# A gated attention and convolution layer on one core: four output tiles summed in one bank, wider evictions, longer parameter rows, and a new written order

## The chip, the core and the metric

The kernel runs on one core of a Trainium2 chip. The core has a matrix engine (TensorE, "PE" in the profile, its weight loads "PEld"), a vector engine (VectorE, "DVE"), a scalar engine (ScalarE, "ACT"), GpSimd ("POOL"), SyncE ("SP", which here only issues transfers) and 16 DMA engines. Matmuls write PSUM, a small memory of 8 banks; VectorE or ScalarE must copy each result out of it (an *eviction*) before the bank can be used again. The metric is the device time of one execution in microseconds; lower is better.

## The reference, cut to what matters

```python
x = A_x                                            # (1, 2048, 512), bf16
g = sigmoid((x * gate_w).sum(-1, keepdims=True))
a = A(x)                                           # attention, 32 heads of 16, four segments of 512 tokens
b = B(x)                                           # long convolution, one filter of 2048 taps per channel
return g * a + (1 - g) * b

# A, segment s:  p = softmax(causal(q k^T / 4));  a_dot = p v
#   num, den = phi(q) M, phi(q) z                  # memory of the earlier segments
#   o = sigmoid(beta) * num / (den + 1e-6) + (1 - sigmoid(beta)) * a_dot
#   M, z += phi(k)^T v, sum phi(k);   A = concat(o) @ wo
# B:  dt = exp(log_dt);  K[d, l] = Re sum_n C B dt exp(dt * (A_re + i A_im) * l)
#   y = irfft(rfft(x, 4096) * rfft(K, 4096))[:2048] + x * Dskip
```

## The kernel before

The convolution is a two-level Fourier transform written as matmuls. `x_level1` (L867) loads x in four parts of 512 KB, one for each group of four residues b of the token number modulo 16, multiplies each of the 16 blocks by a constant matrix in two halves, each half in a PSUM bank of its own, copies each half out (32 evictions of 512 columns), and stores the result to a scratch tensor in DRAM, `scr_Z`. `tail` runs twice, once for each half of the channels ("a", "b"), and for 16 frequency groups t it loads constants and the scratch, does the second level (X), multiplies it by the transform of the filter (K, then Y on VectorE), and transforms back (V). After the 16 groups, `fir` (eight pairs of residues) does the last level and the Dskip term by matmul, and evicts 512 columns a pair into a buffer `cv`. `final` (L1358) makes one output tile per residue b (128 tokens b, b+16, ...): four matmuls of the attention result with wo, then one VectorE instruction that adds `cv` times (1 - g), then the store.

The filter comes from `ssm_prep` (six parameter loads, transposed on the PE and evicted as `prm`, L766; exp, sine and cosine), `ssm_powers` (ten squarings, L816 to L826), and `tables(c)` for four channel groups: products of powers on VectorE (`cmul`, three VectorE instructions a call, L1188, L1191, L1195) and short matmuls ("lag"). The attention goes by segment s and head group hg: `project` (pk, pq), `seg_tokens` (values; L941 sets a column of ones), `seg_state` (the memory), `scores` (five groups of scores a head group; each fills four PSUM banks, and one ScalarE exp of 2048 columns at L1091 reads them), `pv`, and `ophase` (memory read, transposition "oT"). The gate g is folded into the scale of each token's attention result, through `oms` and `einvT`.

Every piece of work is an `op` with an engine; plain copies ("ANY") may go to ScalarE (L226) or VectorE (L227). Almost all matmuls show as L695, and all plain transfers as L222. Nothing is scheduled on the chip: `ORDER` is a string written out by hand or by a planner, and `replay` turns it into one instruction list for each engine:

```python
for w in ORDER.split():
    w = w.split("/")
    order.append((int(w[0].rstrip("av")), "ACT" if w[0][-1] == "a" else "DVE", [int(v) for v in w[1:]]))
```

The number is the op in the order in which `build_graph` makes it, the suffix is the engine of an "ANY" op (a ScalarE, v VectorE), and the numbers after the slashes are the buffer slots or banks that it takes. Each engine works through its list in order; `emit` adds a wait for every operand and for the earlier users of a slot. The transfers of one engine are issued in its order too, so a transfer that waits holds up those behind it. SBUF areas are shared over time: a pool of a later phase waits for the pools that lay there before.

## Time and profile before

| | us |
|---|---|
| three runs: median (lowest to highest) | 313.13 (312.26 to 315.39) |
| the profiled execution | 316.78 |
| its span, first to last instruction | 315.0 |
| PE busy / DVE busy / ACT busy | 275.4 / 268.7 / 260.2 |
| POOL busy | 8.3 |

The rows of a profile are read like this. A group row has the source line, the engine, the operation, output and input, the shape, the count, the busy time, the mean length of one, and the idle time of the engine just before with what ended it. The chain of waits starts at the last instruction and goes back, at each step, to what released it. A window row has, for a stretch of the span, each engine's busy time, the granted clock of the PE, the DMA engines' share and their rate. Lengths are of one instruction from start to end; two that follow each other on ScalarE overlap a little, so the distance from start to start is shorter.

### The profile page before, as it was taken

Reading aid. Unit: us, or ns where it says so; the run is one execution under the profiler, and the core shown is the slowest. Engines: PE = TensorE matmul, PEld = TensorE weight load, DVE = VectorE, ACT = ScalarE, POOL = GpSimd, SP = SyncE. Lnnn points to the kernel's source line nnn. Section 1 sums busy time; section 2 is a strip of 40 time slices with the busy share of each in tenths; the row PEclk is TensorE's granted clock in tenths of the full one; section 3 lists DMA queues with packets and bytes.
Section 4 is the critical chain, followed back from the end, with each engine's and each line's share of the span. In section 5 each row is a group of like instructions: output and inputs, shape, how many; then the busy total and the mean of one; then the engine's idle time right before and its main releaser. Section 6 shows DMA issues by size and latency. Waiting matters only on the chain.

```text
span 315.0 us, 10488 instructions
## 1 busy us (share of the span) xinstructions
PE 275.4 (87%) x4459; PEld 193.6 (61%) x4459; DVE 268.7 (85%) x650; ACT 260.2 (83%) x307; POOL 8.3 (3%) x18
## 2 busy tenths in 40 slices
...
GB/s 182 244 157 88 147 155 207 103 33 35 121 85 191 89 83 103 156 172 91 204 173 193 138 165 198 184 162 214 174 279 191 226 251 218 101 21 2 3 175 93
DMA packets 52289, 45.70 MB, mean 145 GB/s; under 512 B 22337, under 2 KB 47570, under 8 KB 52242
## 3 DMA queue, kind: packets, MB, share of 16 engines
...
q10 hardware_dynamic: 674, 0.16, 0.2%
...
HBM read 26.79 MB, written 6.29 MB: 105 GB/s over the span
## 4 chain that ended last, share of the span: by engine, by line
PE 40%; ACT 28%; DVE 14%; DMA 7%; issue 7%; SPq 3%; ACTq 0%; DVEq 0%
PE psum L695 39%; ACT sb L1091 15%; ACT sb L226 8%; DVE sb L1373 3%; DMA sb<-sb 3%; SPq L222 3%; ACT sb L816 2%; DMA sb<-scr_Z 2%; DMA sb<-in_B_A_im_dram 2%; DVE sb L227 2%; DVE sb L1195 1%; DVE sb L1191 1%; DVE sb L1320 1%; ACT sb L969 1%; DVE sb L1228 1%
## 5 line engine op out<-in xcount | busy, mean ns | idle before, releaser
L695 PE MATMUL psum<-sb 128*128 128x17 bf16 (+15 forms) x4341 | 266.9, 226 | 26.5 <-ACT sb L1091 12.9
L695 PEld LDWEIGHTS psum<-sb 128*128 128x128 bf16 (+5 forms) x4341 | 184.4, 100 | 104.6 <-ACT sb L1091 23.9
L1091 ACT ACTIVATE sb<-psum 128x2048 bf16<-128x2048 f32 x80 | 152.5, 1906 | 9.6 <-PE psum L695 8.7
L226 ACT ACTIVATE sb<-psum 128x512 bf16<-128x512 f32 (+3 forms) x157 | 91.7, 645 | 18.4 <-PE psum L695 17.9
L227 DVE CAST sb<-psum 128x512 bf16<-128x512 f32 (+1 forms) x64 | 43.4, 689 | 14.0 <-PE psum L695 13.7
L1320 DVE TENSOR_TENSOR sb<-sb 128x1024 bf16<-128x1024 bf16 x32 | 21.7, 683 | 5.4 <-ACT sb L226 2.8
L1188 DVE TENSOR_TENSOR sb<-sb 128x512 bf16<-128x512 bf16 (+4 forms) x44 | 24.7, 564 | 0.2
L1191 DVE TENSOR_TENSOR sb<-sb 128x512 bf16<-128x512 bf16 (+4 forms) x44 | 24.6, 562 | 0.2
L1103 DVE TENSOR_TENSOR sb<-sb 128x1024 bf16<-128x1024 bf16 (+1 forms) x40 | 22.5, 577 | 2.4 <-ACT sb L1091 2.4
L1195 DVE TENSOR_TENSOR sb<-sb 128x512 bf16<-128x512 bf16 (+4 forms) x44 | 23.8, 548 | 0.5
L1066 DVE TENSOR_TENSOR sb<-psum,sb 128x256 bf16<-128x256 f32 x32 | 13.3, 419 | 0.5
L1373 DVE SCALAR_TENSOR_TENSOR sb<-sb,psum 128x512 bf16<-128x512 bf16 x16 | 10.6, 740 | 2.3 <-PE psum L695 2.3
L816 ACT ACTIVATE sb<-sb 128x512 f32<-128x512 f32 x18 | 12.4, 686 | 0.0
L1228 DVE TENSOR_TENSOR sb<-sb 128x2048 bf16<-128x2048 bf16 x8 | 9.5, 1221 | 0.1
L227 DVE COPY sb<-psum 128x1024 bf16<-128x1024 bf16 x4 | 2.7, 680 | 7.5 <-PE psum L761 7.5
L1223 DVE TENSOR_TENSOR sb<-sb 128x4096 bf16<-128x4096 bf16 x4 | 9.1, 2282 | 0.0
L969 ACT ACTIVATE sb<-psum 128x512 bf16<-128x512 bf16 x12 | 7.6, 632 | 1.7 <-PE psum L966 1.7
L1063 DVE RECIPROCAL sb<-psum 128x16 f32<-128x16 f32 x32 | 8.0, 251 | 0.9 <-PE psum L695 0.9
L1143 DVE TENSOR_TENSOR sb<-psum,sb 128x512 bf16<-128x512 f32 x12 | 8.3, 688 | 0.3
L1020 ACT ACTIVATE sb<-sb 128x512 bf16<-128x512 bf16 x12 | 7.6, 636 | 0.0
L818 DVE SCALAR_TENSOR_TENSOR sb<-sb 128x256 f32<-128x256 f32 x18 | 7.4, 413 | 0.1
L817 DVE TENSOR_TENSOR sb<-sb 128x256 f32<-128x256 f32 x18 | 7.4, 412 | 0.1
...
## 6 DMA issues: line engine op xcount, KB each, us to landing
...
sb<-scr_Z SPq DMA_DIRECT2D x32, 128.0 KB, 3.1
sb<-sb SPq DMA_DIRECT2D x32, 128.0 KB
...
out_dram<-sb SPq DMA_DIRECT2D x16, 128.0 KB, 1.7
```

The source lines that it names most:

```text
L226: fa = lambda e: e.activation(dst(), src(), ACT.Copy)
L227: fd = lambda e: e.tensor_copy(dst(), src())
L695: mm = lambda e, o_, l, r_, st, sp, **kw: e.matmul(o_, lhsT=l, rhs=r_, start=st, stop=sp, skip_group_check=True, **kw)
L816: op("ACT", ("As", 512), lambda e, sq=sq, Z=Z: e.activation(ap(sq, n=512), ap(Z, n=512), ACT.Square), r=[Z], w=[sq], key=PW[h] + PWS * k)
L1066: op("DVE", ("V1", 256), lambda e: e.tensor_tensor(ap(o1, gi * 16, [[128, 4], [32, 4], [1, 16]]), ap(T, dims=[[68, 4], [17, 4], [1, 16]]), ...
L1091: o = op("ACT", ("Ax", 2048), lambda e, P=P, pT=pT: e.activation(ap(pT, n=2048), ap(P, n=2048), ACT.Exp, scale=0.25), r=[P], w=[pT])
L1103: op("DVE", ("V2", 128 * nb), lambda e, pT=pT, dims=dims: e.tensor_tensor(ap(pT, dims=dims + [[1, 128]]), ap(pT, dims=dims + [[1, 128]]), ...
L1188: op("DVE", ("V2" if n > 1 else "V1", 256 * n), lambda e: e.tensor_tensor(run(tile, ne, dst, 1), run(tile, ne, src, sstep), zz(cl * 512), ...
L1191: op("DVE", ("V2" if n > 1 else "V1", 256 * n), lambda e: e.tensor_tensor(run(t2, n, 0, 1), run(tile, ne, src, sstep), zz(cl * 512 + 256), ...
L1195: op("DVE", ("V2" if n > 1 else "V1", 256 * n), lambda e: e.tensor_tensor(D_(), D_(), ap(t2, n * 128, [[-n * 128, 2], [2 * n, 64], [1, 2 * ...
L1320: op("DVE", ("V2", 1024), lambda e, Y=Y, XAB=XAB, K3=K3: e.tensor_tensor(ap(Y, dims=[[512, 2], [1, 512]]), ap(XAB, dims=[[512, 2], [1, 512 ...
L1373: op("DVE", ("V1", 512), lambda e: e.scalar_tensor_tensor(ap(ou, n=512), ap(cv, (b % 2) * 512, n=512), ap(omgT, b, n=1), ap(P, n=512), ALU ...
```

## The change

1. **Four output tiles in one bank.** For b = 12 to 15 (`DIRECT`) `fir` is left out; `final` first runs the convolution matmuls of both halves into the tile's bank, then the four attention matmuls on top, and one plain copy with the scale (1 - g) writes the tile. It may run on ScalarE or VectorE. So that the scale is right, the gate of these tokens becomes g / (1 - g): `einvT` adds a column of `mkT` (0 for these tokens, 1 for the others) in place of 1.0. `cv` has six slots in place of eight; `ou` has 9 in place of 21, since it no longer reaches into the area of V2a.
2. **Two-bank evictions.** Both halves of a first-level block go to one tile of two neighbouring banks, and one copy of 1024 columns takes them out: 16 evictions in place of 32.
3. **Parameters in 1 KB rows.** Partition p takes the four channels 4p to 4p+3 in one row of 1 KB, where it took four rows of 256 B; the eviction of the transposed parameters puts the channels in order, by reading PSUM with a step.
4. **First x in parts.** The first of the four loads of x becomes four of 128 KB, two from SP and two from ACT.
5. **Smaller edits.** Each `pv` waits for its own part of the values and the ones, not for all four parts. For s = 0 the transposition "oT" writes bf16 to PSUM. `F_EXP` is reordered, so that the filter tables have two products of two in place of one of one and one of three.
6. **New order.** `ORDER` is replaced as a whole (1810 ops where there were 1843); of the copies, 146 go to ScalarE (167 before) and 103 to VectorE (98 before).

```diff
+DIRECT = (12, 13, 14, 15)
...
-8/0 10/4 18/0 12/0 11/4 0/0 13/1 1247/0 6/0 34/4 35/0 28/0/0 29v 37/0 38/1 44/2 9/1 26/0 36/3 45/4 60/1 1265/0/0
+13/0 8/0 10/4 12/1 9/4 213/0 0/0 1250/0 28/4/0 18/0 6/0 1248 29v 1249 34/5 35/0 36/0 37/1 1254/0/0 1255a 44/2 39/3
...
-F_EXP = [1, 2, 3, 4, 5, 6, 7, 8, 258, 260, 262, 264, 516, 520, 772, 776, 1032, 1288, 1544, 1800]
+F_EXP = [1, 5, 7, 3, 6, 4, 8, 2, 262, 260, 264, 258, 516, 520, 772, 776, 1032, 1288, 1544, 1800]
...
-    mkT = cload((pidx // 16) % 2 == 1, "mk", F32, 4, q="POOL")
+    mkT = cload(np.stack([(pidx // 16) % 2 == 1, np.isin(pidx % 16, DIRECT, invert=True)], 1), "mk", F32, 4, q="POOL")
...
-    cvP = mkpool("cv", 2048, 8, 3)
+    cvP = mkpool("cv", 2048, 8 - len(DIRECT) // 2, 3)
...
-    ouP = mkpool("ou", 1024, (T0 - a) // 1024, 3)
-    assert a <= T0, a - T0
+    ouP = mkpool("ou", 1024, (H2 - a) // 1024, 3)
+    assert a <= H2, a - H2
...
-        S.dma(lambda T=T: ap(T, dims=[[128, 4], [1, 128]]), lambda wi=wi: prm[wi].rearrange("(k p) n -> p k n", p=128),
+        S.dma(lambda T=T: ap(T, n=512), lambda wi=wi: prm[wi].rearrange("(p k) n -> p (k n)", k=4),
...
-            S.evac(lambda T=T: ap(T, n=1024), lambda P=P: ap(P, n=1024), 1024, r=[P], w=[T], psum16=True)
+            S.evac(lambda T=T: ap(T, dims=[[512, 2], [4, 128], [1, 4]]), lambda P=P: ap(P, dims=[[512, 2], [1, 128], [128, 4]]), 1024, r=[P], w=[T])
...
-            S.dma(lambda xj=xj: ap(xj, n=2048), lambda qd=qd: bass.AP(x.tensor, x.offset + qd * 2048, [[8192, 128], [1, 2048]]),
-                  524288, w=[xj], key=S.key + qd * XLS - 6)
+            xq = [xj]
+            if qd == 0:
+                xq = [xj.part() for _ in range(4)]
+                for bl in range(4):
+                    S.tag = "xl1l%d.%d" % (qd, bl)
+                    S.dma(lambda xj=xj, bl=bl: ap(xj, bl * 512, n=512), lambda bl=bl: bass.AP(x.tensor, x.offset + bl * 512, [[8192, 128], [1, 512]]),
+                          131072, w=[xq[bl]], key=S.key - 6, q="ACT" if bl > 1 else "SP")
+            else:
+                S.dma(lambda xj=xj: ap(xj, n=2048), lambda qd=qd: bass.AP(x.tensor, x.offset + qd * 2048, [[8192, 128], [1, 2048]]),
+                      524288, w=[xj], key=S.key + qd * XLS - 6)
...
-                for hf in range(2):
-                    P = S.ps()
-                    op("PE", c_pe("F", 512), lambda e, P=P, xj=xj, bl=bl, hf=hf: mm(e, ap(P, n=512), ap(W1T, hf * 128, n=128), ap(xj, bl * 512, n=512), True, True),
-                       r=[xj, W1T], w=[P], acq=[zs], key=S.key + (b4 / 4) * XLS)
-                    S.evac(lambda zs=zs, hf=hf: ap(zs, hf * 256, [[512, 2], [1, 256]]), lambda P=P: ap(P, dims=[[256, 2], [1, 256]]), 512, r=[P], pw=[zs], key=S.key + (b4 / 4) * XLS)
+                P = S.ps(2)
+
+                def f1(e, P=P, xj=xj, bl=bl):
+                    for hf in range(2):
+                        i = mm(e, ap(P, hf * 512, n=512), ap(W1T, hf * 128, n=128), ap(xj, bl * 512, n=512), True, True)
+                    return i
+                op("PE", c_pe("F", 512, 512), f1, r=[xq[bl % len(xq)], W1T], w=[P], acq=[zs], key=S.key + (b4 / 4) * XLS)
+                S.evac(lambda zs=zs: ap(zs, dims=[[256, 2], [512, 2], [1, 256]]), lambda P=P: ap(P, dims=[[512, 2], [256, 2], [1, 256]]), 1024,
+                       r=[P], w=[zs], key=S.key + (b4 / 4) * XLS)
...
-        op("DVE", ("V1", 4), lambda e: e.tensor_scalar_add(g(einvT), g(expT), 1.0), r=[expP[s]], w=[einvP[s]])
+        op("DVE", ("V1", 4), lambda e: e.tensor_scalar(g(einvT), g(expT), ap(mkT, 1, n=1), None, ALU.add), r=[expP[s], mkT], w=[einvP[s]])
...
+        vone = vp.part()
...
-        op("POOL", ("G", 128), lambda e: e.memset(ap(vp, 16, [[17, 128], [1, 1]]), 1.0), pw=[vp])
+        op("POOL", ("G", 128), lambda e: e.memset(ap(vp, 16, [[17, 128], [1, 1]]), 1.0), w=[vone])
...
-            S.evac(lambda tb=tb: ap(vp, tb * 544, [[17, 32], [1, 16]]), lambda P=P: ap(P, dims=[[16, 32], [1, 16]]), 512, r=[P], pw=[pt, vp])
+            S.evac(lambda tb=tb: ap(vp, tb * 544, [[17, 32], [1, 16]]), lambda P=P: ap(P, dims=[[16, 32], [1, 16]]), 512, r=[P], w=[pt])
...
-        vpad[s] = (vp, vparts)
+        vpad[s] = (vp, vparts + [vone])
...
-        op("PE", c_pe("F", *[136] * 8), f, r=[vp, ek, rk], pw=[PS], acq=[Mx[s + 1]])
+        op("PE", c_pe("F", *[136] * 8), f, r=vpad[s][1] + [ek, rk], pw=[PS], acq=[Mx[s + 1]])
...
-            op("PE", c_pe("F", *[17] * (4 * (4 - J))), f, r=[pT, vparts[J], vp], pw=[T])
+            op("PE", c_pe("F", *[17] * (4 * (4 - J))), f, r=[pT, vparts[J], vparts[4]], pw=[T])
...
-        P3 = S.ps()
+        P3 = S.ps(dt=F32 if s else BF16)
...
+                    if s == 0:
+                        i = e.transpose(ap(P3, tb * 128, n=128), ap(T, tb * 128, n=128), ap(ident, n=128))
+                        continue
...
-        S.evac(lambda: ap(oTT[0], hg * 2048 + 512 * s, n=512), lambda: ap(P3, n=512), 512, r=[P3], pw=[pt])
+        S.evac(lambda: ap(oTT[0], hg * 2048 + 512 * s, n=512), lambda: ap(P3, n=512), 512, r=[P3], pw=[pt], psum16=s == 0)
...
-        for e_, k_ in ((0, 0), (1, 1), (3, 2), (7, 3)):
+        for e_, k_ in ((0, 0), (7, 1), (5, 2), (6, 3)):
...
-        fm(2, 0, 1, 1, 1)
+        fm(3, 0, 5, 2, 1)
...
-        fm(4, 0, 1, 3, 2)
+        fm(1, 0, 3, 2, 2)
...
-        fm(8, 1, 2, 4, 8)
-        fm(12, 3, 4, 2, 9)
-        fm(14, 9, 2, 2, 9)
+        fm(8, 4, 1, 4, 8)
+        fm(12, 5, 1, 2, 9)
+        fm(14, 9, 1, 2, 9)
...
+    convs = []
...
+        def conv(e, P, c0, b, st, sp):
+            for kt in range(2):
+                i = mm(e, ap(P, c0, n=256), ap(G2T, kt * 128, n=128), ap(V2, (b * 2 + kt) * 256, n=256), st and kt == 0, False)
+            for kk in range(2):
+                k = 2 * half + kk
+                i = mm(e, ap(P, c0 + kk * 128, n=128), ap(xTT[0], k * 2048 + b, [[16, 128]]), ap(diagT, k * 128, n=128), False, sp and kk == 1)
+            return i
+        convs.append((conv, V2))
...
+            bs = [b for b in (2 * g2, 2 * g2 + 1) if b not in DIRECT]
+            if not bs:
+                continue
...
+            nb = len(bs)
...
-            def f2(e, P=P, b0=2 * g2):
-                for j in range(2):
-                    for kt in range(2):
-                        i = mm(e, ap(P, j * 256, n=256), ap(G2T, kt * 128, n=128), ap(V2, ((b0 + j) * 2 + kt) * 256, n=256),
-                               j == 0 and kt == 0, False)
-                for j in range(2):
-                    for kk in range(2):
-                        k = 2 * half + kk
-                        i = mm(e, ap(P, j * 256 + kk * 128, n=128), ap(xTT[0], k * 2048 + b0 + j, [[16, 128]]), ap(diagT, k * 128, n=128),
-                               False, j == 1 and kk == 1)
+            def f2(e, P=P, bs=bs):
+                for j, b in enumerate(bs):
+                    i = conv(e, P, j * 256, b, j == 0, b == bs[-1])
...
-            op("PE", c_pe("F", *[256] * 4 + [128] * 4), f2, r=[G2T, V2, diagT] + xTT, w=[P], acq=[cv])
-            S.evac(lambda cv=cv: ap(cv, half * 256, [[512, 2], [1, 256]]), lambda P=P: ap(P, dims=[[256, 2], [1, 256]]), 512, r=[P], pw=[cv])
+            op("PE", c_pe("F", *[256, 256, 128, 128] * nb), f2, r=[G2T, V2, diagT] + xTT, w=[P], acq=[cv])
+            S.evac(lambda cv=cv, nb=nb: ap(cv, half * 256, [[512, nb], [1, 256]]), lambda P=P, nb=nb: ap(P, dims=[[256, nb], [1, 256]]), 256 * nb, r=[P], pw=[cv])
...
-        cv = cvs[b // 2]
+        direct = b in DIRECT
+        k = b // 2
...
-            return mm(e, ap(P, n=512), ap(oTT[0], hg * 2048 + b, [[16, 128]]), ap(woT, hg * 512, n=512), hg == 0, hg == 3)
+            return mm(e, ap(P, n=512), ap(oTT[0], hg * 2048 + b, [[16, 128]]), ap(woT, hg * 512, n=512), hg == 0 and not direct, hg == 3)
...
-        op("PE", c_pe("F", *[512] * 3), f, r=[woT] + [oTp[(s, hg)] for s in range(4) for hg in range(3)], w=[P], acq=[ou])
+
+        def fc(e):
+            for half in range(2):
+                i = convs[half][0](e, P, half * 256, b, half == 0, False)
+            return i
+        if direct:
+            op("PE", c_pe("F", *[256, 256, 128, 128] * 2), fc, r=[G2T, convs[0][1], convs[1][1], diagT] + xTT, w=[P], acq=[ou])
+        o = op("PE", c_pe("F", *[512] * 3), f, r=[woT] + [oTp[(s, hg)] for s in range(4) for hg in range(3)], **({"pw": [P]} if direct else {"w": [P], "acq": [ou]}))
...
-        op("DVE", ("V1", 512), lambda e: e.scalar_tensor_tensor(ap(ou, n=512), ap(cv, (b % 2) * 512, n=512), ap(omgT, b, n=1),
-                                                                ap(P, n=512), ALU.mult, ALU.add), r=[P, omgT, cv], w=[ou])
+        if direct:
+            S.evac(lambda: ap(ou, n=512), lambda: ap(P, n=512), 512, r=[P, omgT], w=[ou], scale=lambda: ap(omgT, b, n=1))
+        else:
+            cv = cvs[k]
+            j = [b_ for b_ in (2 * k, 2 * k + 1) if b_ not in DIRECT].index(b)
+            op("DVE", ("V1", 512), lambda e: e.scalar_tensor_tensor(ap(ou, n=512), ap(cv, j * 512, n=512), ap(omgT, b, n=1),
+                                                                    ap(P, n=512), ALU.mult, ALU.add), r=[P, omgT, cv], w=[ou])
...
```

179 lines of the change are left out of this document (89 added, 90 removed).

## The prediction

> **What bounds the kernel now.** I read the stages first: one row for each stretch, with busy time of PE, PEld, DVE, ACT and POOL.
>
> ```profile
> 0.00:24.00 24.00, 17.21 (x131) 10.63 (x131) 15.59 (x47) 16.08 (x30) 6.98 (x16) 1.00 0.79 193
> 24.00:100.00 76.00, 63.11 (x1304) 39.84 (x1304) 75.31 (x199) 75.82 (x93) 0.66 (x1) 0.98 0.46 111
> 100.00:226.00 126.00, 115.33 (x1946) 83.59 (x1946) 105.21 (x251) 106.23 (x127) 0.65 (x1) 0.97 0.56 159
> 226.00:282.50 56.50, 55.59 (x796) 42.50 (x796) 50.08 (x110) 51.62 (x53) 0.00 (x0) 1.00 0.63 185
> 282.50:292.00 9.50, 8.29 (x165) 6.42 (x164) 8.74 (x23) 8.00 (x5) 0.00 (x0) 1.00 0.01 2
> 292.00:309.40 17.40, 15.84 (x124) 10.63 (x120) 13.73 (x25) 2.47 (x2) 0.00 (x0) 1.00 0.32 107
> 309.40:315.00 5.60, 0.00 (x0) 0.00 (x0) 0.00 (x0) 0.00 (x0) 0.00 (x0) 0.55 0.14 48
> ```
>
> From 24 to 100 us VectorE (75.31 of 76) and ScalarE (75.82) are both full: only less work for the two, or an earlier start, moves that stage. From 226 us the PE is full (55.59 of 56.5, then 15.84 of the 16 us up to its end at 308). Between lies a mixed stage: the PE is busy 115.33 of 126 us, and all three engines sometimes wait. So 315 us is a start, 76 us of two full engines, 126 us of PE work with some 11 us of holes, about 82 us of PE, and 5.6 us in which only the last store is left.
>
> What starts it is in the chain of waits (start, length, what):
>
> ```profile
> 0.74 0.52 ACTq L222
> 1.29 0.37 ACTq L222
> 1.69 5.73 DMA sb<-in_B_A_im_dram
> 7.46 1.05 PE psum L761 x8
> 8.54 0.70 DVE sb L227
> 9.26 0.76 DVE sb L783 x2
> ...
> 22.78 0.49 ACT sb L226
> 23.27 1.76 ACT sb L1091
> ```
>
> VectorE does nothing of use before 8.54 us: it waits for the imaginary parameters, third on ACT's queue, 5.73 us under way. The first exp is at 23.27 us; from there ScalarE has no gap.
>
> **The start (parameters, first x, order).** Two rows: the other parameter's transfer (KB, us from issue to landing), and ScalarE's first work, the exp of dt, in the timeline.
>
> ```profile
> sb<-in_B_A_re_dram SPq DMA_DIRECT2D x1, 128.0 KB, 2.3
> ```
> ```profile
> 3.95 0.60 ACT L772 ACTIVATE sb<-psum 128x512 bf16<-128x512 f32 x1 [0.50 <-PE psum L695]
> ```
>
> The real parameters, issued at 0.74 us ahead of everything, land in 2.3 us; the imaginary ones, of the same size and the same 256 B pieces, take 5.73, because 512 KB of x were issued at the same time. The new order issues both at 0.74 us, with x behind them. I take landing at 3.3 us, the identity (second on ACT's queue) half a microsecond later, transposes 1.05 us: 4.9 us. The eviction now reads PSUM with a step (below: 1.1 us in place of 0.70): 6.0. The exp of dt can't be sooner: its 1 KB moves from first to fourth on ACT's queue, so issued near 2.2 us, landed near 4.7 (2.3 again), matmul behind the transposes, exp 0.60: about 6.5. So the first products start near 6.6 us in place of 9.26: **-2.7 us**. VectorE is full from there, so it keeps this.
>
> Bounds: the best is what the first exp could gain. It stands behind the second projection's eviction and, on the PE, behind the transposes of the last parameters, whose load is now queued on SP behind a 512 KB load of x that waits for a free buffer; 18 us is the earliest I can make of that: -5.3. The worst: DMA engines are busy 0.79 of these 24 us, so the later loads (weights, x) may bound as before, and only the two issue slots are won, 0.52 and 0.37: -0.9. ScalarE issues two more transfers, about 0.5 us each, in time in which it idles until 9.7 us; if that cover goes, +1.0.
>
> The Trainium skill (Trainium Kernel Development and Optimization, Key Constraints) says that transfers issued from SP and ACT run on the same 16 DMA engines and that spreading them only saves the issuer's time; by it the parts of x on ACT are worth nothing but slots, and the whole start only about -0.9. The trace has the reason for more beside it: 2.3 against 5.73 us for equal transfers, by what shares the engines.
>
> **Two-bank evictions and other copies.** Rows by shape: ScalarE, then VectorE.
>
> ```profile
> L1091 ACT ACTIVATE sb<-psum 128x2048 bf16<-128x2048 f32 x80 | 152.5, 1906 | 9.6 <-PE psum L695 8.7
> L226 ACT ACTIVATE sb<-psum 128x512 bf16<-128x512 f32 x146 | 85.9, 649 | 13.7 <-PE psum L695 13.2 <-DVE sb L1139 0.2
> ...
> L226 ACT ACTIVATE sb<-psum 128x1024 bf16<-128x1024 bf16 x1 | 1.0, 1042 | 0.0
> ```
> ```profile
> L227 DVE CAST sb<-psum 128x512 bf16<-128x512 f32 x62 | 42.4, 692 | 13.6 <-PE psum L695 13.4
> ...
> L1188 DVE TENSOR_TENSOR sb<-sb 128x512 bf16<-128x512 bf16 x20 | 9.0, 452 | 0.1
> ...
> L970 DVE TENSOR_SCALAR sb<-psum 128x512 bf16<-128x512 bf16 x12 | 5.0, 413 | 0.8 <-ACT sb L969 0.6
> ...
> L1188 DVE TENSOR_TENSOR sb<-sb 128x256 bf16<-128x256 bf16 x8 | 3.3, 410 | 0.0
> ...
> L227 DVE COPY sb<-psum 128x1024 bf16<-128x1024 bf16 x4 | 2.7, 680 | 7.5 <-PE psum L761 7.5
> ...
> L1188 DVE TENSOR_TENSOR sb<-sb 128x768 bf16<-128x768 bf16 x4 | 2.2, 538 | 0.0
> ```
>
> By length a pair on ScalarE goes from 2 x 649 to about 1042 ns. But the stage is full, so what counts is the distance from start to start, and in the chain that is 0.49 us for 512 columns and 1.76 for 2048: 0.83 ns a column, with hardly a fixed part. A 1024 then takes 0.92 against 0.98. Old: 27 on ScalarE, 5 on VectorE: 27 x 0.49 + 5 x 0.69 = 16.7 us. New, 14 and 2: 14 x 0.92 + 2 x 1.2 = 15.3. Together 1.4 us less; shared by two full engines, **-0.6 us** (bounds: 0, and -2.0 by the lengths).
>
> The Trainium skill (ScalarE: Activation LUTs, What ACT_TABLE_LOAD costs) gives 186 ns plus 0.833 ns a column, and 93 ns overlap between neighbours: a saved instruction is worth 93 ns, 1.2 us of ScalarE's time for 13, and the term about -0.9.
>
> The tables: three instructions each of 256 and 768 columns become 512 twice, per table 3 x (410 + 538 - 2 x 452) = 0.13 us, two tables before 100 us. The parameters' eviction loses the fast copy: 680 ns for 1024 bf16 against 692 for 512 f32, so at the pace of a copy without it about 1.1 us (twice 692 ns, 1.4, at most). One is in the start's chain, counted; the other two go to ScalarE, 0.9 each, one more than before, and VectorE has one of 680 ns less. The bf16 "oT" saves 692 - 413 ns in each of the two that now go to VectorE. These small ones cancel: **0** (plus or minus 0.5). The finer waits of `pv` can only release earlier: 0.
>
> **The middle.** Counted in the two orders, V, X and K copies of half b go from ScalarE to VectorE in nine cases net, 9 x 0.69 = 6.2 us; half of it falls before 226 us, where VectorE has 126 - 105 = 21 us free, the rest into 282.5 - 226 - 50.1 = 6.4 us free. The PE's work is the same to the matmul. So the stages keep their length unless holes move:
>
> ```profile
> L695 PE MATMUL psum<-sb 128*128 128x17 bf16 (+13 forms) x1918 | 114.4, 225 | 10.9 <-issue 4.9 <-DMA sb<-scr_Z 2.6 <-ACT sb L1091 1.6
> ```
>
> 10.9 us of holes in 100 to 226 us, the largest named one, 2.6 us, a load from the scratch. The new list has the same sequence of tasks with small swaps. I take **0**, and 3 us either way: more or less one hole of that size.
>
> **The end.** From one timeline:
>
> ```profile
> 291.65 16.19 PE L695 MATMUL psum<-sb 32*128 32x384 bf16 x128 [0.16 <-ACT sb L1091]
> ...
> 297.18 0.60 ACT L226 ACTIVATE sb<-psum 128x512 bf16<-128x512 f32 x1 [3.20 <-PE psum L695]
> 298.70 10.62 DVE L1373 SCALAR_TENSOR_TENSOR sb<-sb,psum 128x512 bf16<-128x512 bf16 x16 [2.31 <-PE psum L695]
> ...
> 306.75 0.64 PEld L695 LDWEIGHTS psum<-sb 128*128 128x128 bf16 x4 [0.33 <-DVE sb L1373]
> ```
>
> The PE ends at 307.84, VectorE's 16 sums at 309.32, 0.66 apart. With four fewer sums (two become copies on ScalarE, two on VectorE) VectorE needs 14 x 0.66, so it no longer bounds: the PE does. The PE's work before the end is unchanged, but after the last head's eviction (297.78) it has 46 attention matmuls and two convolutions (eight matmuls each, 1536 columns against 2048 for a tile's 0.86 us: 0.65) in place of 43: 46 x 0.216 + 1.3 = 11.2 us against 9.3. Before it lies 1.9 us less. As the PE is full there, its end stays; what goes is the lag of VectorE behind it, 1.48 us, down to one sum and its wait, about 0.8: **-0.7 us**. Bounds: 0 and -1.5 (also the wait of 0.33). The load of wo moves behind the last V stores on SP, ahead of the finals by two exps and more: nothing. Nine `ou` slots at 0.66 us each give a store 6 us: nothing.
>
> **The sum.** -2.7 - 0.6 + 0 + 0 - 0.7 = -4.0 us. The profiled execution took 316.78 us (span 315.0), 1.2% over the median of the runs shown; I expect 312.8 for one like it, and take the same -4.0 from the median: **309.1 us**.
>
> **The rivals.** *The start is not kept* (the forecast's first term does not do what it says): loads of weights and x bound the start, or the holes of the middle absorb it. Then -0.9 - 0.6 and little of the rest: 311.5 us. For it: DMA share 0.79. Against it: VectorE's idle 8.5 us is the cause in the chain. *A better middle*: the first exp comes 5 us sooner and a hole of 2.6 goes: 313.1 - 5.3 - 0.6 - 0.7 - 2 = 304.5. *Slower, by banks*: a two-bank tile needs a neighbouring pair free while the scores hold four of the eight banks, and keeps it for 0.92 us in place of 0.49. From 24 to 100 us both engines now wait for nothing; if each of the 13 tiles there stops the stream for x us, the cost is 13x. It beats the 4.0 from x = 0.31, and the kernel is over 1% slower from x = 0.55; at 0.6 it is 316.9. For it: the PE is busy 63.11 of the 76 us there, so it often waits already for banks or data. Against it: a pair frees two banks at once, and there are half as many copies to wait for.
>
> **How the numbers follow.** 1% (3.1 us) is about what a measurement of this kernel tells from no change: its three runs lie 1% apart. Forecast (start kept, 305.5 to 310.5) 0.50; better middle 0.12; start not kept 0.23; slower by banks, or by a worse middle of the same size, 0.15. Below 310.0: most of the first, all of the second: 0.58; within 1%: 0.27; over 316.3: 0.15. Range: the start's best, -5.3, with -0.6, -0.7 and -3 of the middle at one end, 303.5; -0.9 of the start, +1.0 if ScalarE's issues lose their cover, and +3 of the middle at the other, 316. What lies above is the slower rival.
>
> **What would show it.** The first parameter transposes near 3.8 us, the first VectorE product near 6.6, the first exp near 20; from there to the end of the first segment's scores no gap on ScalarE and VectorE; copies of 1024 columns near 1.04 us; the PE full from about 222 us; VectorE's last sum within 1 us of the PE's end. I am wrong if the first exp is not earlier, if ScalarE waits for the PE between 24 and 100 us, or if the holes between 100 and 226 us grow past 14 us.

## The result, and the profile after

The changed kernel takes 312.19 us (median of 20 runs, 309.59 to 314.43), the kernel before 314.2 us beside it. The ratio is 0.9937 (95% interval 0.9910 to 0.9964): 2.0 us, half of the 4.0 that were forecast. Two more comparisons on other chips gave 0.9956 (0.9910 to 1.0001) and 0.9918 (0.9867 to 0.9968). Single executions of one kernel lie up to 8 us apart here (311.96 to 319.82 before), so times are compared over many runs, and where a profile is used, by several. The ratios leave out slow executions, those more than 1.5% above the fastest of the same kernel. The profile of before that the prediction quotes is a long execution (316.78).

The stages of the changed kernel, in the columns of the prediction's first view (stretch; busy PE, PEld, DVE, ACT, POOL; PE clock, DMA share, GB/s), with the end cut where the PE ends:

```profile
0.00:24.00 24.00, 17.06 (x130) 10.42 (x131) 17.36 (x45) 17.44 (x29) 6.88 (x16) 0.86 0.62 172
24.00:100.00 76.00, 61.65 (x1232) 38.24 (x1244) 74.75 (x200) 74.79 (x82) 0.66 (x1) 1.00 0.46 122
100.00:226.00 126.00, 119.07 (x2087) 88.20 (x2096) 112.88 (x268) 110.67 (x129) 0.64 (x1) 0.97 0.60 170
226.00:282.50 56.50, 53.36 (x777) 40.27 (x779) 50.47 (x111) 49.80 (x45) 0.00 (x0) 1.00 0.53 155
282.50:304.00 21.50, 20.90 (x213) 15.41 (x216) 15.32 (x30) 6.27 (x7) 0.00 (x0) 1.00 0.25 82
304.00:310.50 6.50, 0.00 (x0) 0.00 (x0) 0.74 (x1) 0.00 (x0) 0.00 (x0) 0.84 0.17 56
```

Against before, VectorE and ScalarE do 1.77 and 1.36 us more work in the first 24 us, but 0.56 and 1.03 us less from 24 to 100. Over both stretches that is 1.54 us more for two engines, so, counted in the work of these two engines, a lead of 0.8 us at 100 us. In the middle, from 100 to 226 us, they do 7.67 and 4.44 us more. The middle is where the two profiles differ most.

The start, in the changed kernel's timeline (start, length):

```profile
1.15 0.45 ACTq L222 DMA_DIRECT2D sb<-c_ident  x1
...
2.12 0.54 ACTq L222 DMA_DIRECT2D sb<-in_B_log_dt_dram  x1
...
3.91 0.98 PE L761 MATMUL psum<-sb 128*128 128x128 bf16 x8 [0.54 <-DMA sb<-c_ident]
...
4.93 1.23 DVE L227 COPY sb<-psum 128x1024 bf16<-128x1024 bf16 x1 [3.93 <-PE psum L761]
...
6.09 1.43 PE L695 MATMUL psum<-sb 1*128 1x512 bf16 x5 [1.20 <-DMA sb<-in_B_log_dt_dram]
...
6.51 0.60 ACT L772 ACTIVATE sb<-psum 128x512 bf16<-128x512 f32 x1 [2.15 <-PE psum L695]
...
7.14 0.43 DVE L782 TENSOR_TENSOR sb<-sb 128x256 f32<-128x256 bf16 x1 [0.99 <-ACT sb L772]
...
20.72 1.87 ACT L1104 ACTIVATE sb<-psum 128x2048 bf16<-128x2048 f32 x1
```

The parameters no longer bind; dt does: the PE waits 1.20 us for its 1 KB. The first product stands at 7.14 us (9.26 before), the first exp at 20.72 (23.15 in the timeline of before, 23.27 in its chain of waits). In two more profiles of the changed kernel the first exp came at 21.92 and 20.23.

The middle, by the groups of instructions from 100 to 226 us: the PE's group, with its idle time behind the second bar, for the changed kernel in its first profile and in its third:

```profile
L695 PE MATMUL psum<-sb 128*128 128x17 bf16 (+11 forms) x2055 | 117.8, 221 | 6.6 <-DVE sb L1337 2.0 <-issue 1.3 <-DMA sb<-scr_Z 0.9
```
```profile
L695 PE MATMUL psum<-sb 128*128 128x17 bf16 (+9 forms) x2076 | 121.4, 223 | 3.5 <-DVE sb L1337 1.2 <-DVE sb L1077 0.7 <-ACT sb L1104 0.5
```

The holes of the PE were 10.9 us in the row of before, and are 6.6, 4.5 (second profile) and 3.5 us now.

The end, from the changed kernel's timeline:

```profile
282.72 21.23 PE L695 MATMUL psum<-sb 16*128 16x256 bf16 x213 [0.39 <-ACT sb L1104]
...
293.12 0.75 DVE L1408 SCALAR_TENSOR_TENSOR sb<-sb,psum 128x512 bf16<-128x512 bf16 x1 [1.04 <-PE psum L695]
...
302.27 2.48 DVE L1408 SCALAR_TENSOR_TENSOR sb<-sb,psum 128x512 bf16<-128x512 bf16 x3 [1.67 <-PE psum L695]
```

The PE runs with hardly a gap (20.90 us busy of 21.5) to 303.95, and VectorE, which now waits for it, ends at 304.75: a lag of 0.80 us, 1.48 before.

One point compares the two halves of the span fairly. Counted in the two written orders, behind the exp of block C of segment 2, head group 2, both kernels have the same 160,064 columns of matmuls left. It is this row in the timeline of before, and this one after:

```profile
221.71 1.88 ACT L1091 ACTIVATE sb<-psum 128x2048 bf16<-128x2048 f32 x1
```
```profile
216.50 1.88 ACT L1104 ACTIVATE sb<-psum 128x2048 bf16<-128x2048 f32 x1
```

From there to the end of the span it is 93.3 us before and 94.0 after: in these two profiles the last third gained nothing. Within it, the exp of block C of the last segment's head group 1 and the last exp of all, before and after:

```profile
261.65 1.88 ACT L1091 ACTIVATE sb<-psum 128x2048 bf16<-128x2048 f32 x1
...
292.10 1.88 ACT L1091 ACTIVATE sb<-psum 128x2048 bf16<-128x2048 f32 x1 [0.51 <-PE psum L695]
```
```profile
256.33 1.88 ACT L1104 ACTIVATE sb<-psum 128x2048 bf16<-128x2048 f32 x1 [0.51 <-PE psum L695]
...
285.65 1.87 ACT L1104 ACTIVATE sb<-psum 128x2048 bf16<-128x2048 f32 x1
```

The stage between them shrank from 30.45 to 29.32 us, and the tail from the last exp to the end of the span grew from 22.9 to 24.9.

### The profile page after: what moved, and what is told of

It reads as the page before. It is cut to its first block, busy times and chain, and to the rows that moved or that the text cites. A ratio compares the mean times of both kernels' runs of the same rounds, so it can differ in the third digit from the quotient of the medians.

```text
span 310.5 us, 10440 instructions
## 1 busy us (share of the span) xinstructions
PE 272.0 (88%) x4423; PEld 192.6 (62%) x4459; DVE 271.5 (87%) x651; ACT 259.0 (83%) x286; POOL 8.2 (3%) x18
## 4 chain that ended last, share of the span: by engine, by line
PE 38%; DVE 28%; ACT 15%; DMA 12%; issue 3%; SPq 1%; ACTq 0%; DVEq 0%
PE psum L695 37%; DMA sb<-sb 7%; ACT sb L1104 7%; ACT sb L226 4%; DVE sb L1204 3%; DVE sb L227 3%; DVE sb L1211 3%; DVE sb L1207 3%; DMA sb<-scr_Z 3%; DVE sb L1337 2%; DMA sb<-c_DNM 2%; DVE sb L1244 1%; DVE sb L1239 1%; ACT sb L816 1%; DMA sb<-in_B_log_dt_dram 1%
## 5 line engine op out<-in xcount | busy, mean ns | idle before, releaser
L695 PE MATMUL psum<-sb 128*128 128x17 bf16 (+14 forms) x4289 | 261.3, 224 | 27.6 <-ACT sb L1104 7.5
L695 PEld LDWEIGHTS psum<-sb 128*128 128x128 bf16 (+5 forms) x4325 | 182.4, 100 | 103.9 <-issue 21.9
L226 ACT ACTIVATE sb<-psum 128x512 bf16<-128x512 f32 (+4 forms) x134 | 85.4, 671 | 11.8 <-PE psum L695 11.2
L227 DVE CAST sb<-psum 128x512 bf16<-128x512 f32 (+1 forms) x66 | 45.7, 706 | 5.8 <-PE psum L695 5.4
L1204 DVE TENSOR_TENSOR sb<-sb 128x512 bf16<-128x512 bf16 (+3 forms) x44 | 24.3, 553 | 1.3 <-DMA sb<-sb 0.9
L1211 DVE TENSOR_TENSOR sb<-sb 128x512 bf16<-128x512 bf16 (+3 forms) x44 | 24.1, 552 | 0.4
L1207 DVE TENSOR_TENSOR sb<-sb 128x512 bf16<-128x512 bf16 (+3 forms) x44 | 24.0, 549 | 0.3
L229 ACT ACTIVATE sb<-psum,sb 128x512 bf16<-128x512 f32 x2 | 1.4, 688 | 13.2 <-PE psum L695 13.2
L1408 DVE SCALAR_TENSOR_TENSOR sb<-sb,psum 128x512 bf16<-128x512 bf16 x12 | 8.5, 746 | 3.0 <-PE psum L695 2.7
```

Source lines behind the costliest of these rows:

```text
L226: fa = lambda e: e.activation(dst(), src(), ACT.Copy)
L227: fd = lambda e: e.tensor_copy(dst(), src())
L695: mm = lambda e, o_, l, r_, st, sp, **kw: e.matmul(o_, lhsT=l, rhs=r_, start=st, stop=sp, skip_group_check=True, **kw)
L1204: op("DVE", ("V2" if n > 1 else "V1", 256 * n), lambda e: e.tensor_tensor(run(tile, ne, dst, 1), run(tile, ne, src, sstep), zz(cl * 512), ...
L1207: op("DVE", ("V2" if n > 1 else "V1", 256 * n), lambda e: e.tensor_tensor(run(t2, n, 0, 1), run(tile, ne, src, sstep), zz(cl * 512 + 256), ...
L1211: op("DVE", ("V2" if n > 1 else "V1", 256 * n), lambda e: e.tensor_tensor(D_(), D_(), ap(t2, n * 128, [[-n * 128, 2], [2 * n, 64], [1, 2 * ...
```

## The experiments

The ratios are to the kernel before, run on the same chip. "Holes" are the PE's idle time between 100 and 226 us. e3 to e7 were not run beside the changed kernel; they are compared with it by the ratios, and its own three (0.9918 to 0.9956) lie 1.2 us apart.

**e1: the kernel before, a second profile.**

> The kernel before, unchanged, profiled a second time, because its first profiled execution (316.8 us) lay 2.6 us over the median of its runs. Theory (the hole at 195 to 201 us belongs to the kernel): the wait of some 2.6 us of the PE for a load from the scratch is there again, the last exp starts near 292, and the span is 313 to 315. Rival (that one execution had a late load): the wait is under 1 us and the last exp starts near 289.5, so that the 2 us by which the last exps of the changed kernel lie ahead more than its start explains are no part of the change.

```profile
L695 PE MATMUL psum<-sb 128*128 128x256 bf16 (+12 forms) x1954 | 117.7, 226 | 7.9 <-issue 3.1 <-DVE sb L1320 1.3 <-DMA sb<-scr_Z 0.9
```

Neither theory holds whole. The wait for the scratch fell from 2.6 to 0.9 us, but the last exp came at 291.69 and the span was 314.6. The holes together fell by 3.0 us, and the exp with 160,064 columns left came 2.1 us sooner (219.58); but the stretch behind it took 1.7 us longer (95.0 against 93.3). So a hole that one profile names isn't a property of the kernel, and one profile is not enough even for their sum (10.9 and 7.9 in the two of before, 7.1 to 8.5 in the other kernels with the old order below).

**e2: the start, first attempt.** In the kernel before: the 1 KB rows, and the list's head

```diff
-8/0 10/4 18/0 12/0 11/4 0/0 13/1 1247/0 6/0 34/4 35/0 28/0/0 29v
+8/0 10/4 12/0 13/1 0/0 18/0 11/4 1247/0 6/0 28/0/0 29v 34/4 35/0
```

> The kernel before with two edits of the start alone: 1 KB rows of the parameters, and the imaginary parameters first on ACT's queue (the identity second, dt third; their transposes ahead of dt's matmul). Both theories: transposes near 4.5 us in place of 7.5, first exp 1.5 to 2.5 us sooner. Theory (in an unchanged order the start is kept, because both engines are full after it): 1.5 to 2.5 us faster than before, ratio 0.992 to 0.995. Rival (holes between 100 and 226 us give it back, so the start was worth little by itself): within 0.7 us of before, ratio 0.998 to 1.002.

Measured 0.9996 (0.9961 to 1.0031). But the start moved little: now the identity was late (the PE waited for it until 6.07 us), and the first exp came at 22.70. So the run tells little.

**e8: the start as in the changed kernel**, x in four parts behind identity and W1.

```diff
+13/1 12/0 0/0 1250/0 18/0 6/0 1248 1249 1247 8/0 10/4 11/4 28/0/0 29v 34/4 35/0
```

> The kernel before with the start of the changed one as nearly as its order allows: 1 KB rows, imaginary parameters first on ACT's queue, the first x in four parts issued behind the identity and W1 (two on ACT, two on SP), parameter transposes ahead of dt's matmul. Both theories: transposes near 4 us, first exp 1.2 to 2.4 us sooner than 23.15. Theory (a lead gained before 160 us does not last: from 160 to 205 us the PE waits for transfers, so a lead of 1.4 us shrinks to nothing there, as the lag of the split evictions did): ratio 0.997 to 1.002, last exp within 0.7 us of that of the first start experiment (287.8). Rival (the forecast: full engines keep the start): 1.2 to 2.4 us faster than before, ratio 0.992 to 0.996.

Its stages up to 100 us:

```profile
0.00:24.00 24.00, 18.65 (x131) 11.00 (x131) 17.54 (x50) 17.27 (x30) 6.99 (x16) 1.00 0.72 197
24.00:100.00 76.00, 63.87 (x1314) 40.22 (x1315) 75.35 (x201) 75.89 (x95) 0.66 (x1) 0.98 0.46 113
```

The first exp came at 22.26, only 0.9 us sooner. But VectorE and ScalarE do 1.95 and 1.19 us more work before 24 us, as in the changed kernel, and stay full after it, so 1.6 us of lead are there at 100 us. The ratio is 1.0032 (0.9997 to 1.0067), which leaves out the rival's 1.2 us and more; the medians of all runs are 313.67 and 314.09. Of the 1.6 us the time shows at most some tenths. Where they go is not shown: in this profile the exp with 160,064 columns left (217.50) and the last exp (288.14) still lie ahead of those of the four profiles of the old list with the old start (219.4 to 221.7 and 289.4 to 292.1), but three of these four are long executions. The last exp lies within 0.7 us of e2's, as the theory said; that the PE's waits from 160 to 205 us take the lead is not shown by it.

**e3: the parameters in 256 B pieces** in the changed kernel, copied in one piece.

```diff
-              lambda T=T: ap(T, n=512), lambda wi=wi: prm[wi].rearrange("(p k) n -> p (k n)", k=4),
+              lambda T=T: ap(T, dims=[[128, 4], [1, 128]]), lambda wi=wi: prm[wi].rearrange("(k p) n -> p k n", p=128),
```

> The changed kernel with the parameters loaded in 256 B pieces and copied in one piece, as before; order and the rest as changed. Both theories: the parameters land later than in the changed kernel (2.9 us) and the copy falls from 1.23 to 0.69 us, so the first exp moves by less than 1 us either way. Theory (a lead or lag of this size is absorbed from 160 to 205 us): within 0.5 us of the changed kernel, ratio 0.992 to 0.996. Rival (the rows carry part of the gain): 0.7 to 2 us slower than the changed kernel, ratio 0.996 to 1.000.

Measured 0.9948 (0.9907 to 0.9989), as the changed kernel. The copy falls back to the fast form, from 1.23 us:

```profile
5.23 0.69 DVE L227 COPY sb<-psum 128x1024 bf16<-128x1024 bf16 x1 [4.22 <-PE psum L761]
```

The first exp stood at 20.82. The rows carry none of the gain that these runs can tell.

**e4: each two-bank eviction as two instructions.**

```diff
...
+for hf in range(2):
+    i = put(ap(zs, hf * 256, [[512, 2], [1, 256]]), ap(P, hf * 512, [[256, 2], [1, 256]]))
```

> The changed kernel with each of its 16 two-bank evictions of the first transform written as two instructions of 512 columns, one behind the other on the same engine; tiles, order and everything else as changed. Theory (the merged instruction is worth next to nothing): within 0.4 us of the changed kernel, so ratio 0.992 to 0.996 to the kernel before, and ScalarE's and VectorE's busy time up by less than 1 us. Rival (what the forecast took, 0.6 us, or the 93 ns a saved instruction): 0.6 to 1.2 us slower than the changed kernel, ratio 0.995 to 0.998.

ScalarE's groups over the whole span, first the changed kernel, then this one:

```profile
L226 ACT ACTIVATE sb<-psum 128x1024 bf16<-128x1024 f32 x14 | 14.9, 1063 | 0.1
```
```profile
L898 ACT ACTIVATE sb<-psum 128x512 bf16<-128x512 f32 x28 | 16.1, 668 | 0.4 <-PE psum L695 0.4
```

The merged form saves 1.2 us of ScalarE's time. The Trainium skill (ScalarE: Activation LUTs, What ACT_TABLE_LOAD costs) has 186 ns plus 0.833 ns a column and 93 ns overlap; by that, as an estimate, a 1024 takes 1039 ns and 14 saved instructions are worth 1.3 us, and this trace agrees with both (1063 ns, 1.2 us). The ratio is 0.9958 (0.9930 to 0.9987), at the edge of the changed kernel's own (0.9918 to 0.9956): none of it is seen in the time, and 0.6 us is below what these runs can tell.

**e5: without the direct tiles, first placing.** The changed kernel with `DIRECT = ()`, eight `cv` slots; four pairs of convolutions and their copies put back into the list, two pairs ahead of the score matmuls of the last segment's head group 2, block C, and two of the copies on ScalarE.

> The changed kernel without the four direct tiles: their convolutions are computed and copied to SBUF in pairs during the last score stage, as all others, and summed by VectorE at the end; the order is otherwise that of the changed kernel. Theory (the four convolutions, 2.6 us of PE, were moved from a stage in which the PE waits for the exps into a tail that the PE bounds): last exp within 0.7 us of that of the changed kernel, from its start to the span's end 22.5 to 23.2 us in place of 24.85, total 1.2 to 2.2 us under the changed kernel, ratio 0.987 to 0.990 to the kernel before. Rival (the PE is full before the end as the forecast took it): the last exp comes 1.5 to 2.5 us later, and the total stays within 0.6 us of the changed kernel, ratio 0.992 to 0.996.

Measured 1.0243 (1.0192 to 1.0295), outside both. ScalarE's exps and copies in the last stage:

```profile
270.02 1.88 ACT L1104 ACTIVATE sb<-psum 128x2048 bf16<-128x2048 f32 x1 [0.52 <-PE psum L695]
276.26 1.88 ACT L1104 ACTIVATE sb<-psum 128x2048 bf16<-128x2048 f32 x1 [4.36 <-PE psum L695]
...
283.53 0.60 ACT L226 ACTIVATE sb<-psum 128x512 bf16<-128x512 f32 x1 [3.02 <-PE psum L695]
```

The added work sits in front of what ScalarE waits for: 4.36 us ahead of one exp, and a copy that holds up the next exps behind it. This is the price of the place, not of the direct tiles.

**e7: without the direct tiles, second placing**, each addition behind the score matmuls and with a bank free around it.

```diff
-DIRECT = (12, 13, 14, 15)
+DIRECT = ()
```

> The changed kernel without the direct tiles once more, now with the eight added instructions (four pairs of convolutions, four copies, all on VectorE) put where a bank is free for a dozen tasks around, and each behind the score matmuls that ScalarE waits for. Theory (the PE is full from 250 us, so the 2.6 us of convolutions cost the same before the last exp as behind it): last exp 1.5 to 2.6 us later than in the changed kernel, 22.5 to 23.2 us from there to the end in place of 24.85, total within 0.7 us of the changed kernel, ratio 0.992 to 0.996. Rival (the direct tiles moved work out of holes into the tail): last exp within 0.7 us, total 1.2 to 2.2 us under the changed kernel, ratio 0.987 to 0.990. Second rival (the direct tiles save banks and copies that the last stage lacks, as the badly placed version suggests): 1 us or more over the changed kernel, ratio above 0.997.

Measured 1.0048 (1.0011 to 1.0085), the second rival's number. The last exp came 2.63 us later, as the theory said, but the tail shortened by 0.8 us only. ScalarE still waited longer ahead of the last exps than in the changed kernel (6.0 against 2.6 us from 256 us to the last exp), up to

```profile
283.51 1.88 ACT L1104 ACTIVATE sb<-psum 128x2048 bf16<-128x2048 f32 x1 [2.66 <-PE psum L695]
```

So it doesn't separate the tiles from the place either.

**e11: the old end behind the new middle.** Without direct tiles; from the last segment's first head group on, the tasks left stand in the order of before.

```diff
-DIRECT = (12, 13, 14, 15)
+DIRECT = ()
...
```

> The changed kernel up to the last segment's first head group (about 247 us), and from there the order of the kernel before, its choice of engine for the copies and its end: no direct tiles, all convolutions copied in the last score stage, 16 sums on VectorE. Theory (the new end is worse than the old one: the 2.6 us of convolutions lay partly in the PE's waits for exps and now lie whole in the tail): from the third score block of the second head group to the end 53.2 to 53.6 us in place of 54.2, total 0.5 to 1.2 us under the changed kernel. Rival (the direct tiles save banks and copies that the last stage lacks, as the first two versions without them suggest): 1 us or more over the changed kernel.

Measured 1.0104 (1.0063 to 1.0145). From the exp of head group 1, block C, to the end it is 53.4 us (260.43 to 313.85), in place of 54.2, as the theory said. But at the seam ScalarE stood still:

```profile
247.36 1.88 ACT L1104 ACTIVATE sb<-psum 128x2048 bf16<-128x2048 f32 x1 [0.43 <-PE psum L695]
252.15 0.74 ACT L226 ACTIVATE sb<-psum 128x512 bf16<-128x512 f32 x1 [2.39 <-PE psum L695]
...
260.43 1.88 ACT L1104 ACTIVATE sb<-psum 128x2048 bf16<-128x2048 f32 x1
```

The seam cost more than the end gave. And the 0.8 us of the end aren't a gain: at that exp the changed kernel has 2,800 matmul columns more left than the kernel before (86,128 against 83,328), 1.2 us of work at the pace that the prediction quotes, 2,048 columns in 0.86 us. Nothing is lost in the changed kernel's end; the work has moved there.

**e15: the direct tiles alone**, in the kernel before: its order, without the four pairs, the convolutions at the head of those tiles' sums.

```diff
+DIRECT = (12, 13, 14, 15)
-cvP = mkpool("cv", 2048, 8, 3)
+cvP = mkpool("cv", 2048, 8 - len(DIRECT) // 2, 3)
```

> The kernel before with the four direct tiles alone: their convolutions are dropped from the last score stage and computed at the head of each of these tiles' sums, two of the four copied by ScalarE, nine output buffers; order otherwise as before. Theory (the gain of the change is in the middle's order; direct tiles only move work behind the last exp): last exp 0.5 to 2.6 us sooner than 287.8 to 289.4, the tail longer by the same within 0.5 us, ratio 0.998 to 1.003. Rival A (the forecast's end, only VectorE's lag goes): ratio 0.9965 to 0.9985. Rival B (the direct tiles carry the change, as the two versions without them suggest): ratio 0.988 to 0.995.

Measured 1.0035 (0.9984 to 1.0086). Its holes (the matmuls' line is one further down), and its tail from the last exp to the end:

```profile
L696 PE MATMUL psum<-sb 128*128 128x17 bf16 (+11 forms) x2062 | 116.8, 221 | 8.5 <-issue 2.9 <-ACT sb L1092 1.9 <-DMA sb<-scr_Z 0.9
```
```profile
291.27:316.13 24.86, 18.42 (x152) 13.19 (x152) 12.58 (x23) 3.85 (x4) 0.00 (x0) 0.98 0.26 86
```

The tail is 24.86 us, 22.9 before, as in the changed kernel (24.87). This profiled execution (its last exp at 291.27) was a long one, so the stage before the tail isn't read from it. The ratio is a little above the theory's bound and far from rival B's, so the direct tiles by themselves don't carry the gain: rival B is out, and with it the reading of e5 and e7 as what the tiles alone are worth.

**e6: sixteen tables on GpSimd's queue.** Between 190 and 260 us SP is issuing for 7 to 9 of every 10 us.

```diff
...
-lambda t=t: hC[t][:, 1280:2048], 196608, w=[CT], key=kx - 6)
+lambda t=t: hC[t][:, 1280:2048], 196608, w=[CT], key=kx - 6, q="POOL" if half else "SP")
```

> The changed kernel with 16 of SP's transfers, the 192 KB tables of the second half's tail, issued by GpSimd's queue, which is idle there; everything else as changed. SP issues 8 to 9.4 us of every 10 between 190 and 260 us. Theory (the rate at which SP can issue paces the PE's waits for loads from 160 us): SP 1 us of 10 less busy from 170 to 260 us, the waits of the PE for loads and swaps between 160 and 205 us (0.6 to 2.4 us each) fall by half or more, 1 to 2.5 us faster than the changed kernel, ratio 0.986 to 0.991. Rival (the time that a transfer takes to land paces them, whatever queue issues it): within 0.6 us of the changed kernel, ratio 0.992 to 0.996.

```profile
L695 PE MATMUL psum<-sb 128*128 128x17 bf16 (+14 forms) x2146 | 122.1, 221 | 2.6 <-DVE sb L1337 0.6 <-issue 0.5 <-ACT sb L1104 0.3
```

In its profile all waits of the PE for the scratch are gone, the holes are 2.6 us and the span 307.6, as the theory said. But the ratio is 0.9944 (0.9910 to 0.9978), the rival's, and the third profile of the changed kernel itself has a span of 307.3. A single profile would have settled this wrongly.

**e14 and e13: the same tables on GpSimd in the kernel before**, without and with e8's start; the edit is e6's.

> The kernel before with the 16 tables of 192 KB of the second half's tail issued by GpSimd in place of SP. Theory (SP's rate of issue makes the loads from the scratch late, in both kernels): the PE's wait of 0.6 to 2.6 us for the scratch near 200 us is gone, 1 to 2.5 us faster than before, ratio 0.992 to 0.997. Rival (the loads are late for another reason): within 0.6 us of before, ratio 0.998 to 1.002.

> The kernel before with both edits: the changed start (1 KB rows, imaginary parameters first, first x in parts) and the 16 tables issued by GpSimd. By itself that start gave a lead of 0.9 us at the first exp and nothing at the end. Theory (a lead is lost only where SP's transfers pace the PE): with SP relieved the lead lasts, 0.6 to 1.2 us under the kernel with the tables on GpSimd alone, last exp ahead by as much. Rival (the middle absorbs a lead for other reasons too): within 0.4 us of it.

Measured 0.9984 (0.9944 to 1.0023) and 0.9972 (0.9937 to 1.0007), holes 7.6 and 7.5 us. e14's rival holds: issuing from another queue doesn't move the kernel before. In e13 the start is worth 0.4 us by the ratios, the bound of its rival, and 1.3 by the medians (312.67 and 313.93); intervals of more than 1 us either way don't exclude the theory's 0.6 to 1.2.

**e16: all 32 tables on GpSimd** in the changed kernel; the 320 KB ones get the same edit.

> The changed kernel with all 32 tables of the second half's tail (192 and 320 KB) issued by GpSimd. Theory (SP's rate of issue paces the middle): SP 3 us of 10 less busy from 190 to 260, PE's holes between 100 and 226 us 2 to 3 us, 1 to 2 us under the changed kernel of the same call. Rival (no issue rate paces it): within 0.7 us of it.

Measured 0.9930 (0.9887 to 0.9973), beside 0.9918 for the changed kernel on that chip: the rival. The Trainium skill (Trainium Kernel Development and Optimization, Key Constraints) says that transfers from all issuing engines run on the same 16 DMA engines and that issuing from several saves only the issuer's time; the times of e6, e13, e14 and e16 agree within what they can tell. That SP's time bound isn't seen beyond the spread of these runs: the holes of e6, e16 and e17 are the smallest of all (2.6, 2.7 and 3.0 us), and their medians (311.21, 310.95 and 310.01 us) lie under the changed kernel's (311.58 to 312.67), but not clear of the spread.

**e17: dt's load second, and e6's tables.**

```diff
-13/0 8/0 10/4 12/1 9/4 213/0 0/0 1250/0 28/4/0 18/0 6/0 ...
+13/0 8/0 10/4 12/1 9/4 213/0 0/0 18/0 1250/0 28/4/0 6/0 ...
```

> The changed kernel with the 16 tables of 192 KB on GpSimd and dt's 1 KB second behind the identity on ACT's queue, ahead of the parts of x, because the PE waited 1.2 to 2.4 us for dt there. Theory (a lead of the start is lost in the middle, and the tables on GpSimd are worth under 0.6 us): exp of dt 0.5 to 1.5 us sooner, total within 0.7 us of the changed kernel of the same call. Rival (both add up): 1 to 3 us under it.

```profile
5.42 0.60 ACT L772 ACTIVATE sb<-psum 128x512 bf16<-128x512 f32 x1 [1.07 <-PE psum L695]
...
6.22 0.42 DVE L782 TENSOR_TENSOR sb<-sb 128x256 f32<-128x256 bf16 x1
```

dt's exp comes 1.1 us sooner and the first product 0.9 us. The ratio is 0.9916 (0.9879 to 0.9954), median 310.01 us: the lowest of all, but against the changed kernel on the same chip (0.9918, mean 310.96) 0.6 us lower in the mean, give or take 1.2, so not told apart.

**e9 and e10: the changed kernel again**, on the chips of e11, e13, e14 and of e15 to e17.

> The changed kernel, unchanged, beside the three next ones and the kernel before on one chip, since the comparisons across chips differ by about 1 us. Expected as first measured: ratio 0.991 to 0.997 to the kernel before; from the start of the third score block of the last segment's second head group (256.3) to the span's end 54.2 us.

> The changed kernel, unchanged, on one chip with the three next ones. Expected: ratio 0.991 to 0.998 to the kernel before; PE holes between 100 and 226 us 4 to 6.6 us.

Both ratios, 0.9956 and 0.9918, are as expected, and so are the 54.2 us of e9; the holes are 4.5 us in e9 and 3.5 in e10, where 4 to 6.6 were expected.

**e18 and e19: the engines of the copies exchanged.** Beside its sequence, the new list gives 74 of the 217 copies that both kernels share (those of `fir` not counted) to the other engine. e18 puts these back in the changed kernel, e19 moves them in the kernel before; only the suffixes change. Six of e18's, picked out of several lines:

```diff
-31a 221v 219v 104a/4 302v 173a/9
+31v 221a 219a 104v/4 302a 173v/9
```

> The changed kernel, its sequence of tasks kept, with the engine of each of the 74 copies that the two lists give to different engines put back to that of the kernel before. Theory (the sequence fills the PE's holes): holes between 100 and 226 us stay under 7 us, within 1 us of the changed kernel, ratio 0.990 to 0.998. Rival (the choice of engines fills them): holes 7 to 11 us, ratio 0.998 to 1.005. Third case (neither: sequence and engines hold only together): holes as large or larger, and slower than the kernel before, ratio above 1.005.

> The kernel before, its sequence kept, with those 74 copies on the engines that the new list gives them. Theory (the sequence): holes between 100 and 226 us 7 to 11 us as before, ratio 0.998 to 1.004. Rival (the engines): holes 3 to 7 us, ratio 0.990 to 0.996. Third case (only together): holes larger than 11 us, ratio above 1.005.

Measured 1.1335 (1.1251 to 1.1420) and 1.1235 (1.1179 to 1.1291): the third case, by far. The PE's groups from 100 to 226 us, e18 and e19:

```profile
L695 PE MATMUL psum<-sb 128*128 128x17 bf16 (+11 forms) x1868 | 106.0, 223 | 18.7 <-ACT sb L1104 5.0 <-DVE sb L1079 3.1 <-DVE sb L1337 2.9
```
```profile
L695 PE MATMUL psum<-sb 128*128 128x17 bf16 (+12 forms) x2011 | 109.7, 219 | 14.8 <-DVE sb L227 3.2 <-ACT sb L1091 2.6 <-issue 1.7
```

Each of these two sequences is good only with its own engines. The runs can't say which of the two fills the holes; they say that the list is one thing, and that each list here is worth some 40 us against a list with the wrong third of its copies.

**What the runs say together** (e18 and e19 apart). There is a second fair point: behind the exp of block B1 of segment 1, head group 2, the two lists have 309,092 and 309,088 columns of matmuls left. Before and after:

```profile
131.64 1.87 ACT L1091 ACTIVATE sb<-psum 128x2048 bf16<-128x2048 f32 x1
```
```profile
131.54 1.87 ACT L1104 ACTIVATE sb<-psum 128x2048 bf16<-128x2048 f32 x1
```

The seven profiles with the old list reach it at 129.7 to 133.3 us (median 130.5), the eleven with the new list at 130.4 to 134.6 (median 132.6): there, the new list is no longer ahead. From it to the exp with 160,064 columns left both lists do as many columns of matmuls (149,028 and 149,024), and in the first profile of each ScalarE (75.7 and 75.0 us) and VectorE (76.9 and 77.8 us) are busy nearly as long. The old list takes 86.5 to 90.1 us for this stretch (median 87.0), the new one 81.7 to 85.0 (83.6), without overlap, whatever part was undone.

Most of the 3.4 us is idle time of the PE (medians 6.3 and 3.8 us). The rest is the granted clock: in this stretch it is 0.96 to 0.98 in five profiles of the old list, and 1.00 in its other two, e14 and e15, and in all of the new. At that clock the stretch still takes 86.5 and 86.7 us with the old list. Whether the new list has a part in the clock isn't shown.

Behind that exp, kernels with an end of their own list need 93.1 to 95.2 and 93.5 to 94.2 us. So the gain, some 3.4 us less what was lost ahead of it, is made between 132 and 217 us, in the middle. The holes from 100 to 226 us agree: 10.9, 7.9, 7.1, 7.9, 7.5, 7.6 and 8.5 us with the old list, 6.6, 4.5, 3.5, 4.2, 4.0, 2.6, 2.7, 3.0, 4.4, 3.3 and 5.3 with the new one.

The start isn't what makes it: e2, e8 and e13, with the old list and the new rows, need 86.6 to 87.3 us there. Rows, merged evictions and direct tiles aren't either, since the stretch stays at 83.1 to 84.8 us where one of them is undone (e3, e4, e5, e7, e11). What is left is the list and what went in with it in all eleven and was never undone: the finer waits of `pv`, the reordered tables, the bf16 "oT". These are not separated.

## Why the prediction was right or wrong

The sign and the range (303.5 to 316) held; the sum did not: 4.0 us were forecast, 2.0 came. Two steps failed. Full engines were to keep the 2.7 us of the start, and hardly any of it is seen in the time; and the middle was put at 0, and made the gain.

- **The start, -2.7: failed at "VectorE is full from there, so it keeps this".** What was worked out for the first microseconds held: transposes at 3.91 (3.8 forecast), eviction 1.23 us (1.1, at most 1.4), end of dt's exp at 7.11 (6.5; dt was waited for until 6.09, not 4.7, and took the parameters' place as the last to land), first product at 7.14 (6.6), first exp at 20.72 (near 20). But the product was 2.1 us sooner while the two engines had done only 1.6 us more each by 24 us; in the changed kernel their idle time from 24 to 100 us then rose from 0.7 and 0.2 to 1.25 and 1.2 us; and e8, where they stay full and the 1.6 us reach 100 us, is not faster (-0.1 to +2.1 us). The first exp was a poor sign of a lead: the new list puts it ahead of 3,840 more columns of matmuls than the old one (474,228 left behind it against 470,388), and at the fair point near 132 us nothing is left of its 2.4 us. The term measures about 0 in e8, and 0.4 to 1.3 us in e13 against e14; 2.7 lies outside e8's interval. The changed kernel with the old start was not run. The rival "the start is not kept" was right in that; where the lead is absorbed isn't shown. That its price, 311.5, lies 0.7 us from the time is luck: the middle, which it didn't count, paid.
- **Two-bank evictions, -0.6: mechanism right, not seen in time.** Copies of 1024 took 1063 ns (1042 forecast) and ScalarE saved 1.2 us; e4, without the merging, is not slower by anything that can be measured. The two sums given, 0.6 by distances and 0.9 by the Trainium skill's overlap, can't be told apart here.
- **Rows, small copies, 0:** right for the rows (e3). The finer waits, the bf16 "oT" and the tables weren't tried by themselves, so their 0 is open.
- **The middle, 0: mis-sized, and the term that carries the result.** "The new list has the same sequence of tasks with small swaps" took two long lists for nearly the same because the tasks were; a third of the shared copies had changed engine, and e18 and e19 show how much hangs on that. Over as many columns the middle takes some 3.4 us less (87.0 and 83.6), of which 2.6 are idle time of the PE. The holes of the PE fell by some 4 us (means 8.2 and 4.0 of the profiles listed), more than the plus or minus 3 that was given, and the net is 1.4 to 2.6 us by the three ratios. What filled the holes isn't traced to one task, nor to the list apart from the small edits.
- **The end, -0.7: right in its parts, 0 in sum.** The PE bounds the tail and VectorE's lag went from 1.48 to 0.80, as forecast. The stage before gave back 1.1 us (29.32 in place of 30.45), not the 1.9 of the forecast, against 2.0 us of longer tail. From the last point of equal work on, nothing is gained (93.5 to 94.2 us against 93.1 to 95.2); e15, the tiles alone, agrees (1.0035).
- **Slower by banks, 316.9:** ScalarE's idle time from 24 to 100 us grew, but by 1 us over the whole stretch, not by 0.3 or more for each of 13 tiles. **A better middle, 304.5:** its second half, the fewer holes, came true without its first, the start.
- **What would show it:** "if the first exp is not earlier, if ScalarE waits for the PE between 24 and 100 us, or if the holes between 100 and 226 us grow past 14 us". The second happened, in a small way (ScalarE waits 0.47 us for the PE ahead of one exp, at 60.87 us); that the holes shrink was not among them.

Still open: where a lead from the start is lost, and which tasks of the new list, or which of the small edits, fill the holes. Exchanging tasks one by one would need a list planned anew for each, as e5, e7 and e11 show.
